# Strassen's method for a second matrix product, with weight blocks fetched again in every batch

## The chip, the cores and the metric

The kernel runs on one core of one Trainium2 chip. The metric is the device time of one execution in microseconds. Three timed executions of the kernel before took 501.92, 504.31 and 504.30 us: the median is 504.3 us.

## The reference

Eight batches of 576 tokens go through block-wise attention (eight heads of 64, blocks of 64 tokens) and then through a gated MLP. The MLP is what the change touches:

```python
h = x @ w_in                       # 576x512 @ 512x1024, then Gelu
u, v = h[..., :512], h[..., 512:]
v_n = (v - mu) / np.sqrt(var + 1e-06) * g_ln
v_s = np.einsum('ts,bsd->btd', w_sg, v_n) + b_sg[None, :, None]
out = x + (u * v_s) @ w_out
```

Inputs and outputs are float32.

## The kernel before

Every float32 operand of a large matmul is held as a high and a low part, and a product is three matmuls (low by high, high by low, high by high). `split` (line 378) makes the parts: a cast on ScalarE, then a subtraction on VectorE or GpSimd. The weights come as 64-bit words and are decoded at the start (`pair_begin`, `pair_end`, lines 443 to 472, for `w_in`; `o_w`, line 511, for `w_out`).

A batch has four stages on TensorE. **v** (`v_unit`, line 817): four units of 128 tokens, 12 matmuls of 512 columns each, and in even batches a fifth unit for the first 64 tokens of two batches together (`xodd`). Then Gelu, a normalization whose reciprocal root GpSimd computes (tile `sm`), and a split into `v` high and low. **u** (`u_unit`, line 856): four units, each 128 of the 512 output rows, 24 matmuls of 288 columns, then one Gelu on ScalarE straight out of PSUM. **s** (`s_unit`, line 883): the token mix with `w_sg`, 28 matmuls a unit, then VectorE multiplies by u and `g_split` makes the parts. **o** (`o_unit`, line 930, for batches 0 and 1; `o_fast`, line 981, for batches 2 to 7).

`o_fast` is Strassen's method in Winograd's form: the 512x512 by 512x576 product is cut into 2x2 blocks, and seven block products stand in place of eight. Its products (`product`, line 947) use 12 matmuls of 288 columns each. They go, in the order 1, 5, 2, 6, 3, 7, 4, through three PSUM tiles; products 6, 7 and 4 add to what product 1 left in tile `a`, and product 3 to what product 5 left in `b`, so each waits until VectorE has read the tile. Three products (3, 6, 7) take sums of weight blocks as the stationary operand, held in two tiles `wx`; a fourth sum replaces block (1,0) of the weights in place. `w_sums` (line 539) makes them once, beside batch 2's u units: sums on GpSimd, splits on ScalarE and VectorE. The moving operand's sums (`ts`) are made by `g_split` and `late_split`.

Attention runs in between on the same engines: scores (`att_scores`, line 648), transposition (`att_transpose`, line 718: VectorE's block transposition, copies on ScalarE and VectorE into `ptT`) and output (`att_out`, line 745), whose result `keep` (line 788) writes as `xf` (whole), `xh` and `xl` (parts). A tile is 128 tokens; nine tiles are two batches. `SLOTS` (line 64) says behind which unit of a batch a tile's step stands in the program, for odd (1) and even (0) batches: "S" scores, "T" transposition, "O" output. `xh`, `xl` of a batch share two buffers with `gh`, `gl` of the same batch (tags `big_0`, `big_1`).

The order on each engine isn't the order of the program. A planner (`Plan`, line 172) records every operation with a cost (`price`, line 131), gets a due time for each by going back from the matmuls (`due`), simulates the engines three times (`run`), and emits the operations in the order of their simulated starts. All are emitted from one line, so the profile gives line 232 for all; groups are told apart by the tiles' names. In a name `pm<-wsg,v` the left is what is written and the right what is read.

`START` (line 45) is the order of steps for loading and decoding weights and for batches 0 and 1; "D11" and "D14" in it are dummy matmuls (`keep_clock`, line 1051), each of which shows as two records `pm<-ident`. `ON_POOL` (line 70) names steps that run on GpSimd in place of VectorE. `REST_V` and `REST_U` (line 82) choose for each piece of `w_in` where its low part is made: "p" on TensorE, "v" VectorE, "g" GpSimd.

Of the kernel before, what the change touches and what calls it, by code (L numbers as in the profile page):

```python
# [20 lines left out]
PSUM = bass.MemoryType.PSUM  # L21

B, H, S, D = 8, 8, 576, 64
P = 128
# [21 lines left out]
A1 L2 L0 A0 B0 B1 L1 S0 T0 A2 A4 W0 A3 D11 W1 L3 S1 W2 S2 S3 w0 w1 W3 T1 O0 w2 O1 T2 w3 D14 T3 S4 M0 O2 v00 X0 O3 G0  # L46
T4 v01 A8 B8 O4 x0 X1 v02 x1 X2 v03 U1 X3 v04 U0 x2 g0 P5 x3 g2 g3 g4 F0 u02 g1 F1 u03 T5 s00 T6 P7 s01 Q5 s02 T7 T8
s03 Q7 v10 v11 Y0 v12 v13 Y2 Y1 u10 Y3 u11 Y4 s10 Y5 s11 Y6 u13 Y7 u12 A10 B10 s12 P9 A12 s13 T9 T10 o02 P11 A14 o01
o03 o00 Q9 B12 T11 o10 T12 o11 B14 S13 A15 o12 T13 Q11 o13
"""  # L50

SUMS = {5: 0, 6: 1, 7: 2, 8: 3}
# [21 lines left out]
FAST = 2  # L74

# [6 lines left out]
REST_V, REST_U = "pppp", "gggg"  # L82
ENGINES = ("tensor", "vector", "scalar", "gpsimd", "sync")
AHEAD = 96
# [8 lines left out]
def cells(a):  # L93

    width = mybir.dt.size(a.dtype)
# [23 lines left out]
class Op:  # L119
    def __init__(self, engine, method, args, kwargs):  # L120
# [7 lines left out]
        self.locks = False  # L128
        self.cost, self.lag = self.price()

    def price(self):
# [3 lines left out]
        if self.engine == "tensor":  # L135
            x = self.ins[-1]
            n = self.outs[0].free_size()
            if x.dtype == F32R:
                return (5.9 if n < 400 else 4.6) + 0.447 * n, 160
            if x.dtype == BF16:  # L140
                return 4.6 + 0.42 * n, 160
            if self.ins[0].ap[0][1] == D:
                return 40, 160
            return (118 if self.method == "transpose" else 1.83 * n + 10), 160
        if self.engine == "sync":
            return (420 if self.ins[0].ap[-1][1] >= P else 620), 2500 + self.ins[0].size() / 100
        wide = [a for a in self.ins if a.free_size() > 1]
        copies = self.method in ("tensor_copy", "tensor_scalar") and n > 1
        if self.engine == "gpsimd":
            self.locks = self.method == "tensor_tensor" and n > 8  # L150
        if self.engine == "vector":
            if self.method == "memset":
                return 600, 80
            self.locks = not psum and (len(wide) > 1 or copies)
# [4 lines left out]
        return (850 if "pow" in str(self.kwargs.get("op")) else 200 + 1.8 * n), 42  # L159
# [10 lines left out]
class Plan:  # L170

    def __init__(self, nc):
        self.nc, self.ops, self.touched = nc, [], {}
        self.tag_of, self.room, self.order = {}, {}, {}
        for e in ENGINES:
            setattr(self, e, Recorder(self, e))
# [13 lines left out]
    def add(self, op):  # L190
        k = len(self.ops)
        self.ops.append(op)
        seen = [(a, True) for a in op.outs] + [(a, False) for a in op.ins]
# [40 lines left out]
    def due(self, users, after, at):  # L234
# [16 lines left out]
        return late  # L251

    def run(self, users, after, at):
# [17 lines left out]
        def begin(k):  # L271
# [4 lines left out]
            for name in op.tiles:  # L276
# [3 lines left out]
                rank = 0 if name == heads[key][0] else 1  # L280
# [4 lines left out]
            if op.engine == "sync":  # L285
                t = max(t, lanes[0])
            if op.locks:
# [5 lines left out]
        for _ in range(len(ops)):  # L293
            best = None
            for e in ENGINES:
                if e == "tensor":
                    while pe < len(tensor) and start[tensor[pe]] is not None:
                        pe += 1
                    ks = [k for k in tensor[pe : pe + AHEAD] if start[k] is None]
# [33 lines left out]
            if op.locks:  # L333
                held[e] = [t, t + cost + op.lag]
# [29 lines left out]
def block_attention_gated_mlp(ctx: ExitStack, tc: tile.TileContext, qkv, w_in, w_out, w_sg, g_ln, b_sg, out):  # L364
# [11 lines left out]
    ps_m = pool("ps_m", 4, space=PSUM)  # L376

# [150 lines left out]
    def w_whole(blk):  # L528

        r = tmp.tile([P, S], F32, name="r", tag="tmp")[:, : 4 * P]  # L530
        hi, lo = (a[:, blk].rearrange("p k e -> p (k e)").bitcast(F32) for a in (wout_h, wout_l))
        nc.gpsimd.tensor_tensor(r, hi, lo, op=ALU.add)
        return r

    def w_split(place, src):
        hi, lo = (a.rearrange("p k e -> p (k e)") for a in place)
        split(hi, lo, src, nc.scalar, nc.vector)

    def w_sums(step):
        nonlocal wx  # L540
        if step == 0:
            wx = [
                blocks_of(const.tile([P, 3 * 4 * P], F32R, name=f"wx_{i}", tag=f"wx_{i}"), 3) for i in range(2)
            ]
            sums["11"], sums["21"] = w_whole(W_BLOCK[0, 0]), w_whole(W_BLOCK[1, 0])
            s3 = tmp.tile([P, S], F32, name="r", tag="tmp")[:, : 4 * P]
            nc.gpsimd.tensor_tensor(s3, sums["11"], sums["21"], op=ALU.subtract)
            w_split([a[:, 1] for a in wx], s3)
        elif step == 1:
            r = w_whole(W_BLOCK[1, 1])  # L550
            nc.gpsimd.tensor_tensor(sums["21"], sums["21"], r, op=ALU.add)
            nc.gpsimd.tensor_tensor(sums["11"], sums["21"], sums["11"], op=ALU.subtract)
            w_split([a[:, 0] for a in wx], sums["11"])
        elif step == 2:
            r = w_whole(W_BLOCK[0, 1])
            nc.gpsimd.tensor_tensor(r, r, sums["11"], op=ALU.subtract)
            w_split([a[:, 2] for a in wx], r)
        else:
            w_split([a[:, W_BLOCK[1, 0]] for a in (wout_h, wout_l)], sums["21"])
# [35 lines left out]
    wout_h = wout_l = wsg_h = wsg_l = wx = None  # L595
# [52 lines left out]
    def att_scores(*tiles):  # L648
# [29 lines left out]
        for i, t in enumerate(tiles):  # L678
            eng = nc.gpsimd if t > last[1] else nc.vector
# [107 lines left out]

    def keep(b, off, n, src, tiles=0, on_pool=False):
        if b not in xf:
            xf[b] = xp.tile([P, HP, S], F32, name="xf")  # L790
            xh[b] = xp.tile([P, HP, S], F32R, name="xh", tag=f"big_{b % 2}")
            xl[b] = xp.tile([P, HP, S], F32R, name="xl", tag=f"big_{b % 2}")
        dst = [a[b][:, :, off : off + n] for a in (xh, xl, xf)]
# [13 lines left out]
        if off == 0:  # L807
            if b % 2 == 0:
# [314 lines left out]
```

## Time and profile before

| what | value |
|---|---|
| median of three timed executions | 504.3 us |
| profiled execution, its own time | 504.54 us |
| its span, first to last instruction | 502.7 us |
| mean granted TensorE clock | 0.995 |
| ScalarE busy | 288.5 us |
| GpSimd busy | 107.1 us |
| moved by DMA | 46.58 MB, mean 93 GB/s |

In the profile, PE is TensorE's matmuls, PEld its weight loads, DVE VectorE, ACT ScalarE, POOL GpSimd and SP the engine that issues DMAs (SPq its queue). A group's row gives shapes (partitions x elements), a count, the busy time of the group, the mean duration in ns, and the idle time just before with what ended it. A row of the timeline gives start and duration in us. A row of a stretch gives its length, busy time and instructions of each engine, the granted clock, the share of DMA and GB/s.

### The profile page before, as it was taken

What the parts mean: (1) busy time and instruction counts of PE and PEld (TensorE: products, weight loads), DVE (VectorE), ACT (ScalarE), POOL (GpSimd) and SP (SyncE); (2) the same over time, 40 slices, a digit from 0 to 9 for tenths busy, and PEclk for the clock granted to TensorE, in tenths of its full rate; (3) what the DMA queues carried; (4) which work ended last, traced back from release to release, by engine and by line L of the source; (5) the groups of instructions that cost most, each with busy time, mean ns of one, the idle gap of its engine ahead of it and who ended that gap; (6) DMA issues with size and microseconds to landing.
All of it is one profiled execution on the core that took longest, in us unless ns stands there. A gap on an engine that the chain in (4) does not pass through costs nothing.

```text
span 502.7 us, 12445 instructions
## 1 busy us (share of the span) xinstructions
PE 487.9 (97%) x5198; PEld 451.6 (90%) x5198; DVE 383.6 (76%) x696; ACT 288.5 (57%) x493; POOL 107.1 (21%) x110
## 2 busy tenths in 40 slices
PE   6899899999999999999999999999999999999996
PEld 5577799899998899988999899988999899998996
DVE  6979889895996886889657796889658786676056
ACT  4988498734464887447731688348742688313120
POOL 0234405375710311013000131013100131002000
PEclk9999899999999999999999999999999999999999
DMA  8974012221436431325111423425121510020002
GB/s 335 358 204 145 0 43 70 61 84 43 169 112 170 140 90 58 108 72 150 38 50 51 150 42 97 116 73 150 24 63 42 157 23 22 2 72 24 1 1 94
DMA packets 52683, 46.58 MB, mean 93 GB/s; under 512 B 35218, under 2 KB 45458, under 8 KB 52628
## 3 DMA queue, kind: packets, MB, share of 16 engines
q1 hardware_dynamic: 52628, 45.80, 30.0%
q8 instruction: 41, 0.67, 0.6%
q14 instruction: 14, 0.11, 0.1%
HBM read 36.34 MB, written 9.44 MB: 91 GB/s over the span
## 4 chain that ended last, share of the span: by engine, by line
PE 66%; DVE 16%; ACT 9%; DMA 4%; issue 3%; POOL 1%; SPq 0%; DVEq 0%; POOLq 0%; ACTq 0%
PE pm L232 66%; DMA qk<-qkv 2%; DVE nmax L232 2%; ACT L232 2%; DVE u L232 2%; DVE wsg L232 1%; DVE sm L232 1%; ACT pt L232 1%; DMA wout<-w_in 1%; DVE v L232 1%; DVE xl L232 1%; ACT ptT L232 1%; DVE gl L232 1%; DVE hs L232 1%; DVE wout L232 1%
## 5 line engine op out<-in xcount | busy, mean ns | idle before, releaser
L232 PE MATMUL pm<-wsg,v 128*128 128x288 f32 x768 | 108.2, 296 | 0.2 <-DVE v L232 0.2
L232 PEld LDWEIGHTS pm<-wsg,v 128*128 128x128 f32 x768 | 103.9, 189 | 0.8 <-DVE v L232 0.4
L232 POOL TENSOR_TENSOR sm<-sm,neg_half 128x1 f32<-128x1 f32 x36 | 33.9, 942 | 166.0 <-DVE sm L232 164.8
L232 ACT COPY ptT<-blocks 32x256 f32<-32x256 f32 (+1 forms) x93 | 44.4, 477 | 25.9 <-DVE blocks L232 23.9
L232 PE MATMUL pm<-xh,win_l 128*128 128x288 f32 x256 | 56.2, 301 | 1.9 <-ACT u L232 1.9
L232 POOL TENSOR_TENSOR pt<-pt,nmax 128x512 f32<-128x512 f32 x27 | 30.7, 1149 | 119.1 <-DVE nmax L232 116.3
L232 PE MATMUL pm<-xl,win_h 128*128 128x288 f32 x256 | 55.7, 299 | 0.0
L232 PE MATMUL pm<-xh,win_h 128*128 128x288 f32 x256 | 55.5, 299 | 0.0
L232 PE MATMUL pm<-gh,wout 128*128 128x288 f32 x272 | 53.1, 296 | 0.0
L232 PE MATMUL pm<-win_h,xl 128*128 128x512 f32 x128 | 51.6, 403 | 0.8 <-ACT hs L232 0.8
L232 PE MATMUL pm<-win_h,xh 128*128 128x512 f32 x128 | 50.7, 396 | 0.0
L232 PE MATMUL pm<-win_l,xh 128*128 128x512 f32 x128 | 50.7, 396 | 0.0
L232 ACT CAST gh<-u 128x576 fp32r<-128x576 f32 x32 | 21.6, 674 | 50.2 <-DVE u L232 50.1
L232 ACT ACT_TABLE_LOAD x32 | 41.1, 1283 | 10.3 <-DVE pt L232 7.7
L232 PEld LDWEIGHTS pm<-xh,win_l 128*128 128x128 f32 x256 | 41.9, 191 | 3.5 <-ACT u L232 2.3
L232 DVE TENSOR_TENSOR u<-pm,u 128x576 f32<-128x576 f32 x32 | 24.1, 753 | 26.4 <-PE pm L232 26.3
L232 PEld LDWEIGHTS pm<-gh,wout 128*128 128x128 f32 x272 | 42.4, 188 | 0.3
L232 PEld LDWEIGHTS pm<-xl,win_h 128*128 128x128 f32 x256 | 41.7, 191 | 0.0
L232 PEld LDWEIGHTS pm<-xh,win_h 128*128 128x128 f32 x256 | 41.7, 191 | 0.0
L232 PE MATMUL pm<-gl,wout 128*128 128x288 f32 x136 | 35.2, 297 | 0.1
L232 ACT ACTIVATE v<-hs,sm 128x512 fp32r<-128x512 f32 x32 | 23.0, 723 | 20.1 <-POOL sm L232 15.8
L232 ACT ACTIVATE hs<-pm 128x512 f32<-128x512 f32 x36 | 21.4, 598 | 22.6 <-PE pm L232 21.7
(130 smaller groups left out, 965.2 us busy)
## 6 DMA issues: line engine op xcount, KB each, us to landing
qk<-qkv SPq DMA_DIRECT2D x31, 512.0 KB, 4.5
out_dram<-ot SPq DMA_DIRECT2D x31, 288.0 KB, 2.4
av<-qkv SPq DMA_DIRECT2D x116, 64.0 KB, 3.2
wsg<-w_in SPq DMA_DIRECT2D x4, 512.0 KB, 9.5
wout<-w_in SPq DMA_DIRECT2D x4, 512.0 KB, 5.3
st<-w_out SPq DMA_DIRECT2D x8, 256.0 KB, 3.1
qkv_w<-qkv SPq DMA_DIRECT2D x2, 768.0 KB, 8.6
stage<-w_sg SPq DMA_DIRECT2D x5, 288.0 KB, 4.0
```

What stands on the lines that cost most here:

```text
L232: getattr(getattr(self.nc, op.engine), op.method)(*op.args, **op.kwargs)
```

## The change

u's product of batches 2 to 7 is made like o's: `u_fast` replaces the four u units by seven products through three PSUM tiles. x's quarters need sums (`x_sums`, after v units 1, 2 and 3), which lie in buffers of the next batch (tag `big_{(b + 1) % 2}`); so the attention results of the next batch come later, by a new `SLOTS`, and the first 64 tokens of an odd batch are first kept in `xodd` alone (`from_aside` copies them over).

The sums of `w_in`'s blocks are made once ("V0" to "V3" in `START`), those of `w_out`'s beside batch 2's s units in place of its u units. There is one pair of `wx` tiles for both. So both sets are stored to DRAM when they are made (from SP's queue), and from batch 3 on each batch fetches u's set during v and o's set at the start of s (from GpSimd's queue). `START` has another order and no dummies ("D0" issues none); `ON_POOL`, `REST_V`, `REST_U`, `ACT_SOFTMAX` move small steps between engines; the planner gets other costs, limits and some earlier due times.

```diff
-A1 L2 L0 A0 B0 B1 L1 S0 T0 A2 A4 W0 A3 D11 W1 L3 S1 W2 S2 S3 w0 w1 W3 T1 O0 w2 O1 T2 w3 D14 T3 S4 M0 O2 v00 X0 O3 G0
+A1 L2 L0 A0 B0 B1 L1 S0 T0 A2 A4 W0 A3 D0 L3 S1 W1 W2 S2 S3 w0 w1 W3 T1 O0 w2 O1 T2 T3 w3 S4 M0 O2 D0 v00 X0 O3 G0 T4
...
-SUMS = {5: 0, 6: 1, 7: 2, 8: 3}
+SUMS = {9: 0, 10: 1, 11: 2, 12: 3}
+X_SUMS = {1: 0, 2: 1, 3: 2}
...
-SLOTS = {
-    1: "0:O01 0:S23 4:T2 5:T3 6:O23 6:S4 8:T4",
-    0: "0:O4 0:S56 3:T5 4:T6 5:O56 5:S78 7:T7 8:T8 9:O78 9:S9A 14:T9 15:TA",
-}
-ON_POOL = ("Y", "Z", "l0", "l2", "l3", "n2",)
-ACT_SOFTMAX = (0, 2, 4)
+SLOTS = {1: "3:T0 6:S23 6:T1 9:O01 10:T2 12:T3 12:S4 13:O23 14:T4", 0: "0:O4 1:S56 5:T5 7:T6 9:S78 9:O56 11:T7 12:T8 14:O78 14:S9A"}
+ON_POOL = ("Y", "a", "c", "l0", "l3", "l4", "n2",)
+ACT_SOFTMAX = (2, 4,)
...
-REST_V, REST_U = "pppp", "gggg"
+REST_V, REST_U = "vppp", "pgvv"
-AHEAD = 96
+EARLY = {'P11': 2, 'x3': 12, 'Y4': 2, 'Y0': 8, 'O4': -4, 'L3': 3, 'v01': 12, 'v04': -4, 'X3': 1, 'O3': -4}
+AHEAD = 10000
+HORIZON = 25000
...
+            split_to(block(1, 0), sums["21"])
+            kept[kind] = [spare.tile([P, 3 * 4 * P], F32R, name=f"kept_{kind}_{i}") for i in range(2)]
+            for a, c in zip(kept[kind], wx[kind]):
+                nc.sync.dma_start(out=a.bitcast(F32), in_=c.rearrange("p n k e -> p (n k e)").bitcast(F32))
...
+    def w_extras(kind):
+        wx[kind] = extras()
+        for a, c in zip(kept[kind], wx[kind]):
+            nc.gpsimd.dma_start(out=c.rearrange("p n k e -> p (n k e)"), in_=a)
...
+    def x_sums(b, n):
+        def quarter(i, j):
+            return xf[b][:, 2 * i : 2 * i + 2, j * HS : (j + 1) * HS]
+        if not n:
+            tx[b] = [
+                xp.tile([P, 4, 2, HS], F32R, name=f"tx_{i}", tag=f"big_{(b + 1) % 2}") for i in range(2)
+            ]
+        eng = pick("t")
+        new = lambda: tmp.tile([P, 2, HS], F32, name="xs", tag="tmp")
+        put = lambda k, t: split(tx[b][0][:, k], tx[b][1][:, k], t, nc.scalar, nc.vector)
+        if n == 0:
+            t = new()
+            eng.tensor_tensor(t, quarter(0, 1), quarter(0, 0), op=ALU.subtract)
+            put(3, t)
+            eng.tensor_tensor(t, quarter(1, 1), t, op=ALU.subtract)
+            put(0, t)
+            sums["x"] = t
...
+    def u_fast(b, step):
...
+        def done(pm, i, j):
+            nc.vector.tensor_tensor(part(i, j), pm[:, :, :HS], part(i, j), op=ALU.add)
+            nc.scalar.activation(part(i, j), part(i, j), AF.Gelu_apprx_tanh, scale=-1.0)
+        if step == 0:
+            u2[0] = mp.tile([P, KT, S], F32, name="u2", tag="u2")
+            o["a"] = new()
+            product("u", b, 1, o["a"], True)
+            nc.scalar.copy(part(0, 0), o["a"][:, :, :HS])
+            o["b"] = new()
+            product("u", b, 5, o["b"], True)
+            nc.scalar.copy(part(1, 1), o["b"][:, :, :HS])
+        elif step == 1:
+            c = new()
+            product("u", b, 2, c, True)
+            done(c, 0, 0)
+            product("u", b, 6, o["a"], False)
+            nc.scalar.copy(part(0, 1), o["a"][:, :, :HS])
+        elif step == 2:
+            product("u", b, 3, o["b"], False)
+            done(o["b"], 0, 1)
+            product("u", b, 7, o["a"], False)
+            done(o["a"], 1, 1)
+        else:
+            product("u", b, 4, o["a"], False)
+            nc.scalar.activation(part(1, 0), o["a"][:, :, :HS], AF.Gelu_apprx_tanh, scale=-1.0)
...
-        units += [(u_unit, i) for i in range(4)]
+        units += [(u_fast if b >= U_FAST else u_unit, i) for i in range(4)]
...
+            if b > FAST and i == 1:
+                w_extras("u")
+            if b > FAST and i == nv + 4:
+                w_extras("o")
...
+            if b >= U_FAST and i in X_SUMS:
+                sooner(x_sums, b, X_SUMS[i])
```

The other two steps of `x_sums` have one difference and one split each.

More of the change, by code (lines that the diff above doesn't have):

```diff
@@ L153, in price @@
                 return 600, 80
-            self.locks = not psum and (len(wide) > 1 or copies)
+            self.locks = self.waits = not psum and (len(wide) > 1 or copies)
             one = len(self.ins) == 1 and not psum and self.method in ("tensor_copy", "tensor_scalar")
@@ L250, in due @@
                 late[k] = min(late[k], late[s] - ops[s].cost - lag)
-        return late
+        return [t - op.early for t, op in zip(late, ops)]
     def run(self, users, after, at):
@@ L298, in run @@
                         pe += 1
-                    ks = [k for k in tensor[pe : pe + AHEAD] if start[k] is None]
+                    ks, span = [], 0.0
+                    for k in tensor[pe : pe + 150]:
+                        if start[k] is None:
+                            ks.append(k)
+                            span += ops[k].cost
+                            if span > AHEAD:
+                                break
                 else:
@@ L526, in block_attention_gated_mlp, with blocks_h_l @@
     sums = {}
[L528 to L540, printed above, removed]
-        if step == 0:
[L542 to L548, printed above, removed]
+    def blocks_h_l(kind):
+        if kind == "o":
+            return lambda i, j: [a[:, W_BLOCK[i, j]] for a in (wout_h, wout_l)]
+        return lambda i, j: [a[:, 2 * j : 2 * j + 2, 2 * i * P : 2 * (i + 1) * P] for a in (win_h, win_l)]
@@ new lines, in extras, with w_sums, new, whole @@
+    def extras():
+        return [blocks_of(const.tile([P, 3 * 4 * P], F32R, name=f"wx_{i}", tag=f"wx_{i}"), 3) for i in range(2)]
+    def w_sums(kind, step):
+        block = blocks_h_l(kind)
+        def new():
+            return tmp.tile([P, S], F32, name="r", tag="tmp")[:, : 4 * P].rearrange("p (k e) -> p k e", k=2)
+        def whole(i, j):
+            r = new()
+            hi, lo = (a.bitcast(F32) for a in block(i, j))
+            pick("c").tensor_tensor(r, hi, lo, op=ALU.add)
+            return r
+        def split_to(place, src):
+            split(place[0], place[1], src, nc.scalar, nc.vector)
+        if step == 0:
+            wx[kind] = extras()
+            sums["11"], sums["21"] = whole(0, 0), whole(1, 0)
+            s3 = new()
+            pick("c").tensor_tensor(s3, sums["11"], sums["21"], op=ALU.subtract)
+            split_to([a[:, 1] for a in wx[kind]], s3)
@@ L549, in w_sums @@
         elif step == 1:
[L550 to L553, printed above, removed]
+            r = whole(1, 1)
+            pick("c").tensor_tensor(sums["21"], sums["21"], r, op=ALU.add)
+            pick("c").tensor_tensor(sums["11"], sums["21"], sums["11"], op=ALU.subtract)
+            split_to([a[:, 0] for a in wx[kind]], sums["11"])
@@ L806, in keep, with from_aside @@
             nc.scalar.copy(dst[2], src)
-        if off == 0:
-            if b % 2 == 0:
-                xodd[0] = [xp.tile([P, HP, 2 * ODD], F32R, name=f"xodd_{i}", bufs=1) for i in range(2)]
-            c = slice(b % 2 * ODD, (b % 2 + 1) * ODD)
-            for dst, src in zip(xodd[0], (xh[b], xl[b])):
-                nc.scalar.copy(dst[:, :, c], src[:, :, 0:ODD].bitcast(F32))
+        if off == 0 and not aside:
+            for a, src in zip(odd_columns(b), (xh[b], xl[b])):
+                nc.scalar.copy(a, src[:, :, 0:ODD].bitcast(F32))
+    def from_aside(b):
+        for a, c in zip(x_parts(b), [x[:, :, ODD:] for x in xodd[0]]):
+            nc.scalar.copy(a[:, :, 0:ODD], c.bitcast(F32))
+    tx = {}
+    def x_sums(b, n):
[15 more added lines that the diff above has]
+            sums["x"] = t
+        elif n == 1:
+            t = new()
+            eng.tensor_tensor(t, quarter(1, 1), quarter(0, 1), op=ALU.subtract)
+            put(1, t)
+        else:
+            t = sums["x"]
+            eng.tensor_tensor(t, quarter(1, 0), t, op=ALU.subtract)
+            put(2, t)
     vh, vl, vs = {}, {}, {}
@@ L1062, in block_attention_gated_mlp, with sooner @@
     for step in START.split():
+        nc.early = 1000 * EARLY.get(step, 0)
         steps[step[0]](int(step[1:]))
+    kinds = {att_scores: "S*", scores: "S*", att_transpose: "T*", outputs: "O*", x_sums: "X*", w_sums: "W*"}
+    def sooner(f, *args):
+        nc.early = 1000 * EARLY.get(kinds[f], 0)
+        f(*args)
+        nc.early = 0
+    nc.early = 0
     for b in range(2, B):
-        units = [(v_unit, m) for m in range(4 if b % 2 else 5)]
-        units += [(u_unit, i) for i in range(4)]
+        nv = 4 if b % 2 else 5
+        units = [(v_unit, m) for m in range(nv)]
+        units += [(u_fast if b >= U_FAST else u_unit, i) for i in range(4)]
         units += [(s_unit, i) for i in range(4)] + [(o_fast, i) for i in range(3)]
```

115 lines of the change are left out of this document (75 added, 40 removed).

## The prediction

> **What bounds the kernel now.** I read the page's engine lines first, then the busy time by batch, then TensorE's instructions in order of time.
>
> ```profile
> span 502.7 us, 12445 instructions
> PE 487.9 (97%) x5198; PEld 451.6 (90%) x5198; DVE 383.6 (76%) x696; ACT 288.5 (57%) x493; POOL 107.1 (21%) x110
> PEclk9999899999999999999999999999999999999999
> ```
>
> TensorE is busy for 97% of the span and VectorE for 76%. A mean says little here, so I asked for the stretches; the columns are PE, PEld, DVE, ACT, POOL busy, granted clock, DMA share, GB/s.
>
> ```profile
> 0.00:31.20 31.20, 24.23 (x342) 18.25 (x342) 25.72 (x57) 21.61 (x64) 3.43 (x8) 1.00 0.91 316
> 31.20:63.80 32.60, 29.82 (x257) 23.67 (x253) 27.91 (x50) 23.58 (x55) 15.18 (x12) 0.95 0.35 100
> 63.80:130.00 66.20, 66.04 (x673) 62.57 (x673) 55.55 (x105) 42.08 (x74) 31.12 (x35) 1.00 0.24 73
> 130.00:160.20 30.20, 30.20 (x418) 29.27 (x417) 26.41 (x45) 16.05 (x28) 8.52 (x7) 1.00 0.43 135
> 160.20:220.40 60.20, 59.34 (x695) 54.81 (x694) 47.89 (x86) 39.05 (x57) 10.14 (x11) 1.00 0.34 97
> 274.50:334.60 60.10, 59.95 (x707) 55.94 (x706) 47.91 (x86) 36.19 (x54) 10.41 (x11) 1.00 0.34 96
> 334.60:388.60 54.00, 54.00 (x565) 51.35 (x565) 40.06 (x73) 31.92 (x47) 7.83 (x8) 1.00 0.26 72
> 447.00:498.80 51.80, 51.80 (x354) 49.40 (x352) 26.75 (x45) 12.11 (x19) 3.76 (x4) 1.00 0.09 30
> ```
>
> The first two rows are the start, the next two batches 0 and 1; then come batch 2, batch 4 (even, five v units), batch 5 (odd, four) and batch 7. From 63.8 us on TensorE has no idle time to speak of: 59.95 of 60.10 us, 54.00 of 54.00. Removing matmuls there shortens the run, as long as nothing else becomes late. VectorE is next: 47.91 of 60.10 in an even batch, 40.06 of 54.00 in an odd one. My baseline is the profiled execution, 504.54 us (span 502.7 and 1.8 around it); the median of the three timed runs, 504.3, is 0.2 below.
>
> **What is removed.** A u unit is 24 matmuls of 288 columns.
>
> ```profile
> 182.22 0.54 PE L232 MATMUL pm<-xh,win_l 128*128 128x288 f32 x2
> ...
> 191.93 3.35 PE L232 MATMUL pm<-wsg,v 128*128 128x288 f32 x24
> 446.97 0.40 PE L232 MATMUL pm<-win_h,xl 128*128 128x512 f32 x1
> 449.77 1.75 PE L232 MATMUL pm<-ts,wout 128*128 128x288 f32 x12
> 451.36 0.40 PE L232 MATMUL pm<-win_h,xl 128*128 128x512 f32 x1
> ```
>
> Between the first two rows stand three u units, nothing else: 72 matmuls in 191.93 - 182.22 = 9.71 us, 0.135 us each. (A row's own duration overlaps the next matmul; only starts can be subtracted.) The other rows give 449.77 - 446.97 = 2.80 us for a v unit and 451.36 - 449.77 = 1.59 us for one Strassen product of 12 matmuls. Four u units are 96 matmuls; seven products of 12 are 84. So 12 go in each of six batches, 72 in all: again **9.71 us** off TensorE, all on the path.
>
> **What each batch gains on the other engines.** These rows have the same shapes as the added work.
>
> ```profile
> L232 DVE TENSOR_TENSOR u<-u 128x576 f32<-128x576 f32 x18 | 13.6, 754 | 0.2
> L232 DVE TENSOR_TENSOR ts<-u,ts 128x576 fp32r<-128x576 f32 x18 | 13.5, 753 | 0.2
> L232 DVE TENSOR_TENSOR u<-pm,u 128x576 f32<-128x576 f32 x32 | 24.1, 753 | 26.4 <-PE pm L232 26.3
> L232 ACT CAST ts<-u 128x576 fp32r<-128x576 f32 x18 | 11.6, 674 | 23.3 <-DVE u L232 23.3
> L232 ACT ACTIVATE u<-pm 128x576 f32<-128x576 f32 x32 | 20.5, 647 | 10.0 <-PE pm L232 9.7
> ```
>
> VectorE: four differences of x's quarters, four subtractions for their low parts, three additions in u's end: 11 x 0.753 = 8.3 us. ScalarE: four casts of 0.674 and three copies out of PSUM at about 0.647: 4.6 us; the four Gelus stay. In an even batch ScalarE then has 40.8 of about 58.5 us, which TensorE hides. VectorE is the question. Batches 4 and 5 together: 47.91 + 40.06 + 16.6 = 104.5 us of work in 60.1 + 54.0 - 3.2 = 110.9 us, that is 94%. The even one alone has 56.2 in 58.5, but the softmax of the next pair's first tiles is due only in the odd batch's transposes, so some work can slip over. Can VectorE run so densely without holding TensorE up?
>
> ```profile
> 280.50:291.90 11.40, 11.40 (x57) 9.18 (x50) 10.39 (x22) 9.06 (x14) 4.44 (x5) 1.00 0.49 142
> 281.90:298.30 16.40, 16.40 (x204) 14.21 (x203) 15.58 (x33) 13.69 (x21) 5.81 (x6) 1.00 0.32 89
> 324.20:334.60 10.40, 10.25 (x75) 9.70 (x74) 10.10 (x19) 2.64 (x5) 1.56 (x2) 1.00 0.09 30
> ```
>
> It ran at 91%, 95% and 97% here. The last is the o stage, whose seven products pass through the same three PSUM tiles as the new u stage, each waiting for the read of the one before; TensorE lost 0.15 us in it. That is my low end: five loaded batches (2 to 6) x 0.15 = 0.8 us; batch 7 has room. High end: at 91%, 104.5 / 0.91 = 114.8, which is 3.9 us over for a pair, 9.8 us for the five. I take **3.0 us**, nearer the o stage since its products are built the same way. A gain below nothing is excluded: nothing here gets lighter.
>
> x's sums use the buffers where the next batch's attention results went, so those move to the s and o stages (the new SLOTS). They are the same instructions on the same queues, and where VectorE lags the price is already in the 9.8. Their new wait, x's sums needing the whole batch's tokens, ends behind v's second unit, with at least two v units and one product, 2 x 2.80 + 1.59 = 7.2 us, still ahead of the first use.
>
> **Weight blocks.** The sums for u come early, in the stretch of batches 0 and 1, and o's sums move from u's units of batch 2 to its s units.
>
> ```profile
> L232 POOL TENSOR_TENSOR r<-r 128x512 f32<-128x512 f32 x4 | 6.0, 1512 | 0.3
> L232 DVE TENSOR_TENSOR wx<-r,wx 128x512 fp32r<-128x512 f32 x3 | 3.9, 1303 | 0.0
> L232 DVE TENSOR_TENSOR u<-u 128x288 f32<-128x288 f32 x12 | 5.5, 457 | 0.3
> qk<-qkv SPq DMA_DIRECT2D x31, 512.0 KB, 4.5
> qkv_w<-qkv SPq DMA_DIRECT2D x2, 768.0 KB, 8.6
> ```
>
> Eight GpSimd sums at most 1.512 us each (12.1 us) fit the idle GpSimd. Four VectorE subtractions are at most 1.303 us, 5.2 us; in the old run such sums were done before 160 us, so u's take their place there and o's come on top in batch 2: 47.89 + 8.3 + 5.2 = 61.4 us against 60.2 - 1.6 = 58.6, 2.8 us over. Part slips into batch 3: I take **1.0**, bounds 0 and 2.8. Four stores of 768 KB go on SP's queue, ahead of qk and v loads; each holds the transfer engines for up to 8.6 us, but the loads are issued two tiles ahead. I take 0; without that cover one qk load would be late by up to 8.6.
>
> From batch 3 on, GpSimd's queue issues two 768 KB loads for u, later two for o. They wait for the last product that reads the old blocks; behind them wait v's reciprocal roots, and behind those ScalarE's v, due only in the s stage. For u they must land before product 6: four v units (11.2), the last o product and three u products (4 x 1.59 = 6.4) make 17.6 us, 20.4 in an even batch. No GpSimd load is in this trace. By the SP rows the pair takes 9 us (as two qk loads, quicker for being smaller) to 17.2 us (two of 768 KB one after the other, in the crowded start). I take 12, hidden: 0.
>
> **Start and batches 0 and 1.** "Z" moves 16 sums of 256 columns from GpSimd to VectorE, at most 0.457 us each, 7.3 us: 62.9 of 66.2 us in that stretch. Hidden, 0; at 91% density it would cost 2.9. The start has this wait:
>
> ```profile
> L232 PE MATMUL pm<-ident 128*128 128x128 f32 x50 | 9.1, 335 | 2.4 <-ACT ident L232 2.4
> 31.25 0.50 PE L232 MATMUL pm<-win_h,xl 128*128 128x512 f32 x1
> 52.81 2.33 POOL L232 TENSOR_TENSOR sm<-sm,neg_half 128x1 f32<-128x1 f32 x1 [2.16 <-DVE sm L232]
> 55.17 0.72 ACT L232 ACTIVATE v<-hs,sm 128x512 fp32r<-128x512 f32 x1 [3.72 <-POOL sm L232]
> 56.48 0.54 PE L232 MATMUL pm<-xh,win_l 128*128 128x288 f32 x2 [1.91 <-ACT u L232]
> 54.50:61.40 6.90, 4.99 (x26) 4.85 (x26) 5.42 (x14) 3.56 (x6) 2.17 (x3) 0.75 0.00 0
> ```
>
> The first v unit begins at 31.25. Later a slow root on GpSimd delays ScalarE, which delays TensorE by 1.91 us, and then the granted clock is 0.75 over 6.90 us: 1.7 us more. The new order, with less of the weights' low parts on GpSimd (REST_U), may remove these 3.6 us. Against it: the 25 dummies (50 records) kept the clock up in the first 31 us. They fill waits, so taking them out gains nothing; without them the first v unit may run at half clock, 2.80 us more, and three or four more VectorE operations there at about 0.75 cost up to 3.0. I take **-1.0**, bounds -3.6 and +5.8.
>
> [...]
>
> **Sum:** 504.54 - 9.71 + 3.0 + 1.0 - 1.0 = **497.8 us**, own range 493.5 to 501.5.
>
> **Rivals.** *VectorE becomes the bound* (91% reached, not 95): 504.54 - 9.71 + 9.8 + 1.0 - 1.0 = 504.6, no change. For: it must stay as dense over whole batches as it was over 16 us. Against: TensorE's end of each stage leaves slack, and 97% was seen. Worse density (88%) gives 104.5 / 0.88 - 110.9 = 7.9 per pair, 19.7 in all, 514.
>
> [...]
>
> *All is hidden and the start's wait goes*: 504.54 - 9.71 + 0.8 - 3.6 = 492.0. *The start loses what the batches gain* (+5.8 and 2.9 there): 497.8 + 6.8 + 2.9 = 507.5, or about half of it, 502.7: no change.
>
> **How the numbers follow.** A difference under 0.5% (2.5 us) can't be told from none. Chances: forecast 0.52, all hidden 0.14, VectorE bound 0.18 (0.12 of it no change, 0.06 slower), blocks late 0.10 (slower), start 0.06 (no change). Faster 0.66, same 0.18, slower 0.16. The range 491.5 to 506 leaves out the late blocks, the dense tail and a little below.
>
> **What would show it.** Right: TensorE at 12 fewer matmuls per batch, an even batch near 58.5 to 59.5 us and an odd one near 52.5 to 53.5, VectorE at 92 to 96% of them, product 6 of u waiting for no DMA. Wrong: TensorE idle before u products with a release by VectorE or ScalarE (density), by DMA on wx (late blocks), or a first v unit much after 31 us (start).

## The result and the profile after

The changed kernel takes 508.34 us (median of 20 executions, 504.24 to 515.6); the kernel before, 503.93 us in 20 executions beside it (501.92 to 505.48). The ratio is 1.0083 with the interval 1.0063 to 1.0103: 0.8% slower; it leaves out the two slowest executions of the changed kernel (512.42 and 515.6), which lie over 1.5% above its quickest. The forecast was 497.8 us, 10.5 us too low; the range ended at 506.

The profiled execution of the changed kernel is the quickest of the 20, 504.24 us. Its page first; the last two rows are DMA issues (KB each, median us from issue to landing).

```profile
span 502.3 us, 12336 instructions
PE 478.3 (95%) x5069; PEld 436.9 (87%) x5076; DVE 434.2 (86%) x785; ACT 308.5 (61%) x520; POOL 109.4 (22%) x120
PE 41%; DVE 38%; ACT 8%; DMA 8%; issue 3%; POOL 1%; SPq 0%; DVEq 0%; ACTq 0%; POOLq 0%
out_dram<-ot SPq DMA_DIRECT2D x31, 288.0 KB, 2.5
wx<-kept_u POOLq DMA_DIRECT2D x10, 768.0 KB, 7.1
```

The matmuls went: 5069 in place of 5198, which is 72 of u, 50 records of the dummies and a few records that are missing. But TensorE now idles more, VectorE rose from 76% to 86%, and 8% of the chain that ended last is DMA. Next the stretches that answer to those of the prediction: the start, batch 2, batch 4, batch 5, batch 7.

```profile
0.00:27.60 27.60, 15.49 (x246) 10.36 (x250) 21.39 (x45) 14.96 (x41) 3.01 (x8) 1.00 0.73 267
155.80:218.90 63.10, 60.38 (x684) 54.05 (x681) 56.22 (x98) 43.45 (x68) 21.88 (x18) 1.00 0.41 133
272.90:332.70 59.80, 58.77 (x694) 54.26 (x693) 53.74 (x96) 39.93 (x63) 11.19 (x13) 1.00 0.43 131
332.70:387.60 54.90, 53.64 (x554) 50.10 (x553) 47.91 (x86) 34.22 (x51) 10.80 (x13) 1.00 0.46 146
446.10:498.60 52.50, 50.88 (x342) 47.98 (x340) 35.21 (x60) 17.65 (x28) 5.68 (x8) 1.00 0.29 95
```

The start won 3.65 us here (first v unit at 27.60, before at 31.25). Batch 2 lost 2.9. Batches 3 to 7 should each have shrunk by 1.62 us (12 matmuls of 0.135) and didn't: batch 4 went from 60.1 to 59.8, batch 5 from 54.0 to 54.9, batch 7 from 51.8 to 52.5. TensorE lacks about 1.3 us in batch 5 and 1.6 in batch 7, where it lacked nothing before. From the first v unit of batch 3 to the end of batch 7 it is 279.6 us, before 278.4.

In batch 7 the trail can be followed. It begins with a wait that is on no list of suspects in the prediction: VectorE waits for an output store. First the stores (SP's queue) of this stretch in the changed kernel, in the view of one tile.

```profile
L242 SPq DMA_DIRECT2D out_dram<-ot x4: 372/386/401, 445.4 to 457.3; - x4
  DVE ot L242: 3.0, 1
DMA to landing us min/median/max: 2.2/2.4/8.4
```

The same view of the kernel before:

```profile
L232 SPq DMA_DIRECT2D out_dram<-ot x3: 372/373/401, 446.4 to 452.3; - x3
DMA to landing us min/median/max: 2.2/2.2/2.3
```

And the changed kernel in order of time (start, us, engine, instruction, idle before it and what ended it), GpSimd, VectorE and TensorE:

```profile
446.32 1.12 POOL L242 DMA_DIRECT2D wx<-kept_u  x2 [11.91 <-PE pm L242]
452.75 0.75 DVE L242 TENSOR_TENSOR tx<-xs,tx 128x576 fp32r<-128x576 f32 x1
456.49 0.76 DVE L242 TENSOR_TENSOR ot<-pm,xf 128x576 f32<-128x576 f32 x1 [2.99 <-DMA out_dram<-ot]
464.15 1.87 PE L242 MATMUL pm<-tx,wx 128*128 128x288 f32 x12 [0.27 <-ACT u L242]
468.90 1.87 PE L242 MATMUL pm<-tx,wx 128*128 128x288 f32 x12 [1.29 <-ACT u L242]
```

At 446.32 GpSimd issues the two fetches. A store of batch 6's output goes out on SP's queue just behind them and lands after 8.4 us in place of 2.2. Its source is one of four `tmp` buffers, which x's sums, v's Gelu output, the attention's blocks and the o stage's results share. So VectorE, which needs a buffer for `ot` at 453.5, stands for 2.99 us. VectorE's later operations are late too, ScalarE's behind them, and seven and twelve microseconds on, products 6 and 7 of u wait for ScalarE's copy out of their PSUM tile, 1.56 us together. (Over the whole run VectorE waits for such stores twice, 4.6 us, and ScalarE twice, 3.3 us; in the run without a fetch, below, neither does.) The fetched blocks themselves were there in time:

```profile
L242 POOL DMA_DIRECT2D wx<-kept_u x2: 535/563/591, 446.3 to 446.9; - x2
DMA to landing us min/median/max: 5.9/7.4/8.9
```

The second landed 8.9 us after 446.9, at 455.8; product 6 began at 464.15.

### The profile page after: what moved, and what is told of

Read it like the earlier page. It is cut to its first block, busy times and chain, and to the rows that moved or that the text cites. A ratio compares the mean times of both kernels' runs of the same rounds, so it can differ in the third digit from the quotient of the medians.

```text
span 502.3 us, 12336 instructions
## 1 busy us (share of the span) xinstructions
PE 478.3 (95%) x5069; PEld 436.9 (87%) x5076; DVE 434.2 (86%) x785; ACT 308.5 (61%) x520; POOL 109.4 (22%) x120
## 4 chain that ended last, share of the span: by engine, by line
PE 41%; DVE 38%; ACT 8%; DMA 8%; issue 3%; POOL 1%; SPq 0%; DVEq 0%; ACTq 0%; POOLq 0%
PE pm L242 39%; DMA out_dram<-ot 6%; DVE u L242 5%; DVE nmax L242 4%; DVE sm L242 4%; DVE ot L242 3%; DVE hs L242 3%; DVE v L242 3%; DVE tx L242 3%; DVE xs L242 2%; DVE pt L242 2%; PE banks L242 2%; DVE blocks L242 2%; DVE ptT L242 2%; DMA av<-qkv 1%
## 5 line engine op out<-in xcount | busy, mean ns | idle before, releaser
L242 POOL TENSOR_TENSOR sm<-sm,neg_half 128x1 f32<-128x1 f32 x36 | 30.9, 858 | 133.8 <-DVE sm L242 124.7
L242 ACT COPY ptT<-blocks 32x256 f32<-32x256 f32 (+1 forms) x93 | 44.2, 475 | 23.4 <-DVE blocks L242 21.6
L242 PE MATMUL pm<-win_h,xl 128*128 128x512 f32 x128 | 51.8, 405 | 0.0
L242 DVE TENSOR_TENSOR u<-pm,u 128x576 f32<-128x576 f32 x50 | 36.8, 747 | 13.0 <-PE pm L242 12.5
L242 DVE TENSOR_TENSOR ot<-pm,xf 128x576 f32<-128x576 f32 x32 | 23.9, 748 | 9.9 <-DMA out_dram<-ot 3.0
L242 DVE BATCH_NORM_STATS2 sm<-hs 128x6 f32<-128x512 f32 x36 | 24.7, 686 | 6.4 <-ACT hs L242 6.4
L242 PEld LDWEIGHTS pm<-win_h,xh 128*128 128x128 f32 x128 | 24.0, 188 | 5.9
L242 PEld LDWEIGHTS pm<-win_h,xl 128*128 128x128 f32 x128 | 24.0, 188 | 5.4
L242 PEld LDWEIGHTS pm<-win_l,xh 128*128 128x128 f32 x128 | 24.1, 188 | 4.9
L242 PE MATMUL pm<-xh,win_l 128*128 128x288 f32 x112 | 27.9, 296 | 0.0
L242 PE MATMUL pm<-xl,win_h 128*128 128x288 f32 x112 | 27.9, 296 | 0.0
```

The source lines that it names most:

```text
L242: getattr(getattr(self.nc, op.engine), op.method)(*op.args, **op.kwargs)
```

## The experiments

**What the fetch costs.** Theory: the fetches hold up the stores behind them, the stores hold buffers. Rivals: VectorE's density; late blocks. The first run emits no fetch and lets products 3, 6 and 7 of batches 3 to 7 read the blocks that batch 2 left, so u's weight sums are replaced by w_out's; the order of all else is kept. The second issues u's fetches behind the batch's first reciprocal root on GpSimd's queue.

```diff
 no_fetch, in Plan.emit:
+    if op.method == "dma_start" and op.engine == "gpsimd":
+        continue
+    if op.resident is not None:            # matmuls of products 3, 6, 7
+        op.args = (op.args[0], op.resident, *op.args[2:])
...
 late_fetch, in Plan.emit:
+    if op.method == "dma_start" and op.engine == "gpsimd" and "kept_u" in op.kwargs["in_"].tensor.name:
+        held.append(op)
+        continue
...
+    if op.engine == "gpsimd" and op.kwargs.get("op") == ALU.pow:
+        for x in held:
+            self.nc.gpsimd.dma_start(**x.kwargs)
```

> Left out: the fetch of the weight blocks in batches 3 to 7; products 3, 6 and 7 there read the blocks of w_out made in batch 2, for u as well, so the sums are of other data. The order of all other instructions is the changed kernel's. Stores theory: stores go back to 2.3 us, VectorE no longer waits for a store, 496 to 501 us, and the spread of the runs falls from 6 us to about 2. Density theory (VectorE at 92 to 95% is too dense, the fetch is hidden): 505 to 509, spread unchanged.

> u's two fetches are issued behind the reciprocal root of the batch's first v unit, some 6 us later, in place of ahead of it; all else in the same order. Stores theory: the batch's last stores are out before the fetch, 498 to 503 us. Density theory: no change, 505 to 509. Late-block theory (the fetch itself is awaited): slower, 510 to 515, since it lands later.

Without the fetch: 500.84 us, ratio 0.9931 (0.9912 to 0.995). Batches 3 to 7 last 53.23, 59.29, 53.22, 57.40 and 50.32 us, 273.5 together, 6.1 less than in the changed kernel. Counted from the start of each of TensorE's matmuls to the next one's start, most of this lies in the u stages: 56.7 us for the five, 62.1 in the changed kernel. The result is in the range of the stores theory, and the executions lie within 1.5 us of each other. Issued later: 503.35 us, 0.9979 (0.9958 to 1.0), 0.35 us above that theory's range. Batches 3 to 6 are then as without a fetch, but batch 7 is 52.72: there the last store still comes behind the fetch, lands after 6.8 us, and u's products wait 1.88 us.

Is it the buffers, or the traffic? A fifth `tmp` buffer decides it, with the fetch left where it was and the order planned for four.

```diff
...
-    tmp = pool("tmp", 4)
+    tmp = nc.pool(ctx.enter_context(tc.tile_pool(name="tmp", bufs=5)), 4)
...
-    low = [const.tile([P, P], BF16, name=f"low_{i}") for i in range(2)]
+    low = 2 * [const.tile([P, P], BF16, name="low")]
...
-    g_bc = const.tile([P, DH], F32, name="g_bc")
+    g_bc = win_h[:, 0, DH:].bitcast(F32)
...
```

> The changed kernel with five buffers for the shared temporary tiles in place of four, the order of instructions as planned for four; the room comes from leaving out the normalisation's gain (a row of w_in's weights stands in for it) and one of the two scaled unit matrices, so the values are wrong. Stores theory (the fetch hurts because the stores behind it hold buffers that VectorE and ScalarE need): batches 3 to 7 within 0.4 of those without a fetch (53.2, 59.3, 53.2, 57.4, 50.3), median 500 to 502 with the late rise of the clock. Rival (the fetch hurts through the memory's traffic, or through late blocks): as in the changed kernel, 54.0, 59.8, 54.9, 58.5, 52.4, median 507 to 509.

Measured 502.06 us, 0.9958 (0.9933 to 0.9983). Its stores between 443 and 460 us:

```profile
DMA to landing us min/median/max: 2.3/3.3/8.4
```

VectorE's instruction that had waited 2.99 us, now without a wait:

```profile
451.50 0.75 DVE L244 TENSOR_TENSOR ot<-pm,xf 128x576 f32<-128x576 f32 x1
```

And batches 3, 5 and 7:

```profile
222.20:275.40 53.20, 53.20 (x554) 50.03 (x553) 49.10 (x88) 32.89 (x51) 10.99 (x13) 1.00 0.46 144
334.70:387.90 53.20, 53.20 (x554) 50.08 (x553) 48.05 (x86) 32.91 (x50) 10.80 (x13) 1.00 0.48 151
445.50:495.90 50.40, 50.36 (x342) 47.92 (x340) 35.29 (x60) 17.88 (x28) 5.68 (x8) 1.00 0.30 99
```

A store still takes 8.4 us, but VectorE no longer waits 2.99 us for it. Its first addition in u's end, at 464.08, begins 18.6 us after the batch's first v unit; in the changed kernel, at 467.74, 21.6 us. TensorE is full, and batches 3 to 7 last 273.7 us, within 0.2 of the run without a fetch. The fetch's transfers cost nothing; the buffers held by the delayed stores cost all of its 6 us. This is shown. Why a store is slow behind a fetch is not: no run here separates the ways in which two queues could share the transfers. In the five profiles of the changed kernel each output store that was issued within 1.1 us behind the second fetch, and whose landing is on record, landed 0.2 to 0.8 us behind that fetch. In the first of them there are three, issued at 274.63, 334.40 and 447.96 us: they took 7.1, 8.5 and 8.4 us and landed 0.6, 0.2 and 0.6 us behind it.

**Does the same fetch hurt without the new u stage?** The new start and planner with the old u units were run alone, and then with w_out's blocks stored and fetched again in batches 3 to 7.

```diff
 start_alone, against the changed kernel:
-U_FAST = 2
+U_FAST = 8
 (old SLOTS, old SUMS, no V steps, no w_extras)
 fetch_alone, against start_alone:
+            if b > FAST and i == 1:
+                w_extras("o")
```

> The new start, planner and small moves alone: u of batches 2 to 7 by the old units, the old places of attention and of w_out's sums, no fetch and no stores of blocks. If the 4.4 us that the first profile shows gained before batch 2 are the start's own: 499 to 501 us. If they are only borrowed (work pushed into later batches): 503 to 505.

> u by its old units; the new start, prices and planner as in the run with the start alone, plus w_out's sums stored once and fetched again (two of 768 KB, GpSimd's queue) once in each of batches 3 to 7, at the place of u's fetch. Stores theory: the output store issued behind the fetch lands after 5 us or more in place of 2.3, VectorE or ScalarE waits for its buffer; how much reaches TensorE is open, since plain u units take no tmp buffers: 0.2 to 1.2 us a batch, median 505 to 510. Rival (the fetch costs only because u's products wait on the copies that the buffers hold up): 503.5 to 505.

The start alone: 504.15 us, 0.9994 (0.9975 to 1.0014), as expected of a gain that is only borrowed: in its profile batch 2 begins 1.1 us earlier than before and lasts 1.6 us longer. With the fetch: 503.28 us, 0.9996 (0.9974 to 1.0018), though a store lands after 7.2 us there too.

```profile
L245 SPq DMA_DIRECT2D out_dram<-ot x4: 372/386/401, 271.6 to 280.4; - x4
DMA to landing us min/median/max: 2.2/3.7/7.2
```

No engine is listed as waiting for it; here are no x sums that want a buffer, and no products of u that hang on VectorE. The stores theory expected 505 to 510 here and missed; the rival had it. So the cost needs both parts of the change, the fetch and the new u stage.

**Has VectorE any reserve?** In the run without a fetch, the four subtractions for x's low parts were emitted twice in batches 3 to 7 (3.0 us each), and the four for w_out's sums twice in batch 2.

```diff
+                for _ in range(op.times):   # 2 for these subtractions
                     getattr(getattr(self.nc, op.engine), op.method)(*op.args, **op.kwargs)
```

> The kernel without a fetch (products 3, 6 and 7 of u read w_out's sums in batches 3 to 7, which leaves u's values wrong), with the four VectorE subtractions for the low parts of x's sums done twice in batches 3 to 7 (3.0 us more VectorE work in each), and the four for w_out's sums done twice in batch 2 (about 5 us more). Density theory: VectorE binds the steady batches, so each grows by 1.5 to 3 us and the median is 508 to 516. Slack theory: VectorE's density costs nothing there, each grows by under 0.4, 500.8 to 502.8 if batch 2 is unchanged too. For batch 2: if its extra 2.7 us come from VectorE's sums, it grows from 62.8 by 2 us or more; if from the order of other work, by under 0.7.

519.23 us, 1.0316 (1.0284 to 1.0347): slower than even the density theory expected. From the list of TensorE's waits (us in total, times, longest; the same row of the changed kernel has 3.8 us, and the run without a fetch, on which this one builds, has no such row):

```profile
PE pm L248 <- ACT u L248: 12.0, 6, 2.8
```

Batches 3 and 5 of the same run:

```profile
224.60:280.60 56.00, 53.58 (x555) 50.14 (x554) 52.10 (x92) 33.29 (x51) 8.58 (x9) 1.00 0.26 79
343.00:399.40 56.40, 53.82 (x555) 50.15 (x554) 50.89 (x90) 34.03 (x51) 8.58 (x9) 1.00 0.30 87
```

3.0 us more VectorE work made these batches 2.7 to 3.2 us longer, by the same wait that the changed kernel shows, though VectorE is busy for 93% and 90% of them. Nearly all of it lies in the u stage, 11.4 us without the added work and 13.9 and 14.3 with it. Batches 6 and 7 grew by 5.4 and 3.7 us, 6.8 and 3.4 us of them at half clock, though VectorE is busy for only 71% of batch 7. At its present load it costs nothing there (53.20 of 53.20 above), but ahead of u's products it has no reserve: what it loses there, TensorE loses. So a 3 us wait for a buffer could come through.

**How late may the fetch be, and do dummies help the start?** The changed kernel with eleven dummies at TensorE's front, nothing else altered; and the same with u's fetch behind the batch's second root.

```diff
-A1 L2 L0 A0 B0 B1 L1 S0 T0 A2 A4 W0 A3 D0 L3
+A1 L2 L0 A0 B0 B1 L1 S0 T0 A2 A4 W0 A3 D11 L3
```

> The changed kernel with the first eleven dummy matmuls put back at TensorE's front and nothing else altered. Clock theory (without dummies TensorE runs at half clock until about 18.8 us in some executions and 27.5 us in others, worth 3.4 us): the granted clock is full before 10 us, the first v unit begins at 27.0 to 28.0 in every execution, batches 0 to 7 last as in the changed kernel, and the median is 503.5 to 505.5 with a narrow spread. Rival (eleven dummies at the front don't hold the clock over the idle gaps that follow): the median stays at 507 to 508.5 and the spread stays wide.

> The eleven dummies, and u's two fetches issued behind v1's root on GpSimd's queue, so behind the batch's last output store; else the changed kernel. Stores theory with clock theory: no output store waits behind the fetch, batches 3 to 7 last as without a fetch (62.8 for batch 2 stays; 53.2, 59.3, 53.2, 57.4, 50.3 to 50.8), the fetches land before product 6 needs them, the first v unit begins at 27.0 to 28.0: median 497 to 499.5, faster than both kernels. Late-block theory: u's product 6 or 3 waits for a DMA on wx, a microsecond or more in batches 3, 5 and 7. If the dummies do nothing: 500.5 to 501.5.

509.31 us, 1.0117 (1.0082 to 1.0153), and 511.71 us, 1.0161 (1.0136 to 1.0186): the clock theory failed in the first and the stores theory in the second. In the first the clock was full from 6.7 us, but fell to half again from 13.5 to 20.3. In the second run the rival of late blocks came true in batches 3 and 5 (58.4 and 57.6 us). TensorE in batch 3:

```profile
241.45 0.37 PE L247 MATMUL pm<-tx,wx 128*128 128x288 f32 x1 [1.66 <-DMA wx<-kept_u]
243.41 1.98 PE L247 MATMUL pm<-tx,wx 128*128 128x288 f32 x11 [1.58 <-DMA wx<-kept_u]
```

The stretch behind it:

```profile
244.60:248.00 3.40, 3.40 (x16) 3.40 (x15) 0.00 (x0) 1.83 (x3) 0.57 (x1) 0.50 0.00 0
```

3.2 us of waiting, and then 3.4 us at half clock, which cost 1.7 more, as much as the half clock of batch 0 in the prediction; and this with the fetch two roots behind the place where the change issues it. Batch 3 took 58.4 us where it took 53.2 with the fetch behind the first root: between too early for the stores and too late for product 6 lies one root.

Next both groups of dummies, round which the planner moves some steps of the start; and the same with the fetch behind the first root, in batch 7 behind the second.

```diff
-A1 L2 L0 A0 B0 B1 L1 S0 T0 A2 A4 W0 A3 D0 L3 S1 W1 W2 S2 S3 w0 w1 W3 T1 O0 w2 O1 T2 T3 w3 S4 M0 O2 D0 v00 X0 O3 G0 T4
+A1 L2 L0 A0 B0 B1 L1 S0 T0 A2 A4 W0 A3 D11 L3 S1 W1 W2 S2 S3 w0 w1 W3 T1 O0 w2 O1 T2 T3 w3 S4 M0 O2 D14 v00 X0 O3 G0 T4
```

> The changed kernel with both groups of dummies put back in START (eleven at the front, fourteen ahead of the first v unit; the planner moves some steps of the start round the second group). Clock theory: with the second group the granted clock stays full from about 6.5 us on, the first v unit begins at 27.5 to 28.8 us in every execution, and the median is 504 to 506. Rival (the new order of the start leaves gaps that no group of dummies covers): half clock again between 12 and 27 us, median 508 or more.

> Both groups of dummies, and u's two fetches issued behind v0's root in batches 3 to 6 and behind v1's root in batch 7. Stores theory with clock theory: 497.5 to 500, faster than both kernels. If the dummies don't hold the clock: 501.5 to 504. If the fetch is late behind v0's root already: TensorE waits on wx in batch 3 or 5.

511.16 us, 1.015 (1.0119 to 1.0181), and 508.21 us, 1.0086 (1.0058 to 1.0114): the rival again in the first, and above every figure expected in the second. There batches 4 to 6 are as without a fetch (59.3, 53.2, 57.5), but batch 3 is 0.8 us longer (54.1), batch 7 1.1 us (51.4), and batch 2 took 65.9 us in place of 62.8, with 6.8 us at half clock; against the run without a fetch the start and batch 0 lost 2.8 us together. Two stretches of the start in the kernel before, and the longest wait of TensorE in them:

```profile
6.40:13.00 6.60, 5.05 (x108) 3.06 (x108) 5.27 (x12) 3.16 (x18) 0.00 (x0) 1.00 1.02 414
13.00:20.00 7.00, 4.84 (x80) 3.17 (x78) 6.62 (x16) 6.95 (x25) 0.00 (x0) 1.00 1.00 338
9.96 1.13 PE L232 MATMUL pm<-wsg,ident 128*128 128x512 f32 x2 [1.49 <-DVE wsg L232]
```

And in the kernel with both groups:

```profile
5.50:12.40 6.90, 3.28 (x110) 2.85 (x108) 3.91 (x8) 1.03 (x2) 0.00 (x0) 1.00 1.02 415
12.40:26.00 13.60, 9.22 (x100) 5.42 (x89) 11.46 (x22) 8.18 (x27) 0.98 (x1) 0.50 0.53 196
11.31 0.66 PE L242 MATMUL banks<-ident,first_pts 128*128 128x128 f32 x4 [3.62 <-DVE first_pts L242]
16.38 1.01 PE L242 MATMUL pm<-wsg,low 128*128 128x512 bf16 x2 [3.70 <-ACT win_h L242]
```

In the old kernel TensorE is busy for 77% and 69% and the clock stays full; with the dummies in the new order it is busy for 48%, and half clock follows for 13.6 us. The means hide another difference: it stands still for 3.62 us in one piece just ahead of the fall and for 3.70 us soon behind it, where the old kernel never waits longer than 1.49 us. The first v unit then began at 38.3 us; batch 0 is 4.2 us shorter in return. START of the kernel before, dummies and all, did worse under the new planner; the second of these runs has the edit of the last experiment too.

```diff
-START = """ the changed kernel's """
+START = """ that of the kernel before, V0 V1 V2 V3 behind o01 """
```

> The changed kernel with START of the kernel before, dummies and all (u's four weight sums behind step o01). Clock theory (the old order of the steps and its dummies hold the clock; the new order holds it neither with dummies nor without): full clock from about 6.5 us on, the first v unit at 30.5 to 31.5 us, batches 2 to 7 as in the changed kernel, median 506 to 508.5 with a spread under 3 us. Rival (chance alone): half clock again after 12 us in some executions, spread as wide as the changed kernel's.

> Both edits: results stored in place, and START of the kernel before. Both theories: batches 3 to 7 as without a fetch, the start as in the kernel before, 499.5 to 501.5 with a spread under 3 us. If the old start alone loses the clock too: 501 to 505.

518.75 us, 1.0248 (1.0203 to 1.0294), and 509.01 us, 1.0083 (1.0052 to 1.0113), both above every figure expected: half clock for 17.1 us of the start in both, and again at the end of batch 1 (6.8 and 3.4 us). In the first run the wait for `first_pts` is the same 3.62 us, so under the new planner the old START doesn't bring the old order back.

**Why is the median 4 us above the profiled execution?** The changed kernel was timed once more and profiled three more times, unchanged.

> The changed kernel once more, unaltered, for a second profile beside the quickest of its runs. All theories: 504 to 511 us, median about 508. Stores theory: in a slower run the output stores issued just behind the 1.5 MB fetch at a batch's start take longer than the 7 to 8.5 us of the first profile, and TensorE's idle time in u grows with them. Density theory: the stores take the same, and the extra time lies in VectorE's own chain.

> The changed kernel as it is, one profiled execution more. Clock theory: the first v unit begins either at 27.4 to 28.2 us (full clock from about 19 us, 504 to 505.5 in all) or at 30.5 to 31.5 us (full clock from 26 to 28.5 us, 507 to 509.5), and the batches after it last the same within 1 us. Rival (the executions above 507 lose their time in the batches): the first v unit at 27.5 us in all.

> As the look before: one of the two starts, and the time follows it.

> As the two looks before: one of the two starts, and the time follows it.

Timed again: 507.74 us, 1.0072 (1.0043 to 1.0101). The three further profiled executions took 508.73, 506.37 and 507.47 us. The same two matmuls of the start, and then the first v unit, in the second and in the third of them:

```profile
21.31 1.12 PE L242 MATMUL pm<-wsg,ident 128*128 128x512 f32 x2
27.61 0.48 PE L242 MATMUL pm<-win_h,xl 128*128 128x512 f32 x1
```

```profile
22.54 2.07 PE L242 MATMUL pm<-wsg,ident 128*128 128x512 f32 x2
30.50 0.48 PE L242 MATMUL pm<-win_h,xl 128*128 128x512 f32 x1
```

Same instructions, same order, and 1.12 against 2.07 us: by the trace's record of the clock it became full at 18.8 us in the one and at 26.4 in the other (before its first entry the views print 1.00). That is worth 2.9 us. Of thirteen profiled executions with this start and no dummies, four rise at 18.8 to 20.1 us and nine at 26.3 to 28.2. The rest of the spread is batches 3 to 7: 281.5, 282.2 and 280.0 us in the three (279.6 in the first profile), and in two of them batch 3 alone took 56.4 and 56.6. So theory and rival each had a part.

**Batch 2.** The four subtractions for w_out's sums on GpSimd, in the kernel with the fetch behind the first root:

```diff
+                if op.lows:
+                    op.engine = "gpsimd"
```

> The kernel with u's fetch behind v0's root, with the four subtractions for the low parts of w_out's sums on GpSimd in place of VectorE (batch 2), the order as planned. VectorE theory of batch 2: it shrinks from 62.85 to 60 to 61.3 us, the other batches as before, median 501 to 502.3. Rival (the moved attention steps and sums wait on other things): 62.3 or more, or longer if GpSimd's sums now come late, median 503 to 505.

503.14 us, 0.9987 (0.9963 to 1.0011), and batch 2 took 63.6 us, not 62.85: no gain. With VectorE's subtractions doubled it took 65.4 instead of 62.8. It was 61.8 with the start alone, 60.2 before. So 1.6 us came with the new planner's assignment and order, and 1.0 net with u's products there. The stages, counted as above, say where: u takes 11.3 us in place of 13.0, as forecast, but v 15.8 in place of 14.2 and s 16.7 in place of 15.1, s already 16.6 with the start alone. VectorE has a share, but which part of the 2.6 us that these add is its, stays open. In the second run with the old START batch 2 took 59.3 us, and batch 1 74.6 in place of 70.3, 3.4 us of it at half clock: part of the extra can move ahead of batch 2.

**A version that beats both.** If the delayed stores hurt only by the buffers that they hold, the o stage needs none: its results can be added into `xf` in place and stored from there.

```diff
     def o_part(pm, base, ot=None, es=slice(0, 2)):
         if ot is None:
-            ot = tmp.tile([P, 2, HS], F32, name="ot", tag="tmp")
+            ot = base
```

> The changed kernel with the o stage's results added into the batch's own x tile and stored from there, so that no store holds a buffer of the shared temporary tiles; the planner orders the rest anew. Stores theory: stores still land after 5 us or more behind a fetch, VectorE doesn't wait for them, batches 3 to 7 last 53.2, 59.3, 53.2, 57.4 and 50.3 us or less, median 499 to 502 as with a fifth buffer, faster than both kernels. Rival (the fifth buffer helped by more room for the other tiles): batches 3 to 7 stay within 0.3 of 54.0, 59.8, 54.9, 58.5, 52.4, median 506 to 508.

499.49 us (498.51 to 502.49), ratio to the kernel before 0.9917 (0.9891 to 0.9944). Its stores between 442 and 450 us, and then its batches 5 and 7:

```profile
DMA to landing us min/median/max: 2.3/3.6/8.3
```

```profile
332.00:385.20 53.20, 53.20 (x553) 50.04 (x553) 48.67 (x86) 32.98 (x50) 12.04 (x13) 1.00 0.50 153
442.90:493.70 50.80, 50.62 (x342) 47.95 (x340) 35.52 (x60) 18.08 (x28) 5.68 (x8) 1.00 0.30 98
```

The stores are as slow as ever, and the change pays: 0.8% faster than before, with the early fetch and without dummies. Batches 3 to 7 last 274.6 us, 1.1 more than without a fetch; ScalarE now waits for stores of `xf` itself, 3.9 us in two places.

## Why the prediction was wrong

**Removed matmuls, 9.71 us:** right.

**VectorE's density, +3.0:** right in size, by luck. Without the fetch's cost, batches 3 to 7 gained 278.4 - 273.7 = 4.7 of 8.1 us; 3.4 are lost. But VectorE doesn't hold TensorE up there: with the fifth buffer TensorE idles in neither batch 3 nor 5, and batch 7, which has no attention beside it, gained 1.5 of 1.62. Counted by stages, batch 5's u went from 13.0 to 11.4 us, all that was forecast, while the same matmuls of s took 0.2 us more, those of o 0.3 and those of attention 0.3. So the loss lies in the stages into which the attention steps moved. The prediction had put their price into VectorE's. What makes those matmuls longer wasn't tested. The rival of VectorE as the bound was wrong as stated, but near: ahead of u's products there was no reserve.

**Fetched blocks, 0: the step that failed.** The prediction put this term at 0 because the blocks land before product 6 needs them. They did: 9.5 us after the first issue in batch 7, where it had taken 12. It didn't ask what else is in flight beside them, whose source those transfers hold, and who needs it. That cost 6.0 us (279.6 against 273.7), more in the slower profiles. For the four stores of the blocks it had asked which loads they delay; for the fetch it had named only what is queued behind it on GpSimd. The output stores go by SP's queue, and still landed behind it, by 0.2 to 0.8 us.

**Batch 2, +1.0 (0 to 2.8):** mis-sized, and outside its bounds. It should have been 60.2 - 1.6 = 58.6 us without extra work; it was 62.9 with a fifth buffer, 4.3 more. 1.6 of this the start and the planner add alone; the sum had no term for them in batch 2.

**Start, -1.0 (-3.6 to +5.8):** -1.6 in most executions, inside its bounds, and -4.4 in the first profile, past the lower one; the reason was partly foreseen. Without dummies half clock holds until 18.8 to 20.1 us or 26.3 to 28.2; the first v unit comes at 27.5 to 28.2 or 30.5 to 31.2 (before: 31.25), so the start gains 3.1 to 3.8 us or 0.1 to 0.8, and batches 0 and 1 another 0.8. The wait of 1.91 us in batch 0 and the half clock behind it are gone, as hoped, but batch 0 is only 0.3 us shorter in the first profile: work that stood ahead of the first v unit now stands in it. The half clock ended ahead of the first v unit, so the 2.80 us feared for it weren't paid. That the dummies had kept the clock up in the kernel before was an estimate: no run took them out there. In the new order eleven of them gave full clock from 6.7 us on, but half clock from 13.5 to 20.3, and both groups half clock from 12.4 to 26.0.

With the measured sizes: 504.5 - 9.7 + 3.4 + 4.3 + 6.0 - 1.6 (late rise) = 506.9, and 504.1 with the early rise, against 504.24 profiled and 508.34 in the median; the rest of the median fits the fetch's larger cost in the later profiles, 0.4 to 2.6 us more in batches 3 to 7.

## What to carry to other kernels

When a change adds a large transfer, list every small transfer that will be in flight beside it, and for each the buffer that it holds and the engine that wants the buffer next; the large one may be hidden and still stop an engine through a small one, as here VectorE for 2.99 us. A result that can be stored from a tile with a long life should not sit in a shared temporary. An engine at 90%, or even 71%, in the mean can have no reserve in one stage: double one of its operations there and see whether the stage grows by as much.

## What the runs showed of the hardware

A store of 288 KB took 2.2 to 2.3 us in the kernel before (446.4 to 452.3 us), and 7.1 to 8.5 us in the changed kernel's first profile when issued on another queue 0.9 to 1.1 us behind the second of two fetches of 768 KB (6.6 to 9.6 us over all profiles).

The clock's rise in the start differed between executions of the same program by 7.6 us (18.8 and 26.4). The stretches between two changes of the clock are multiples of 3.413 us: 51.20, 3.41 and 440.32 us in the kernel before (15, 1 and 129 times), 484.69 us in the changed kernel's first profile (142 times), and the stretches of half clock named above last 3.4, 6.8, 13.6 and 17.1 us. So one can ask how busy TensorE was in the last 3.41 us before a fall, and in such windows that kept full clock. Two of the kernel before, a kept one and the one ahead of its fall at 57.6 us:

```profile
13.26:16.67 3.41, 2.02 (x67) 1.66 (x65) 3.16 (x8) 3.36 (x12) 0.00 (x0) 1.00 1.06 415
54.22:57.63 3.41, 1.50 (x10) 1.15 (x9) 2.14 (x4) 2.31 (x5) 0.91 (x1) 1.00 0.00 0
```

Behind the window of 59% the clock stayed full, behind the one of 44% it was half for 3.41 us. The fall after the 1.66 and 1.58 us waits followed a window of 46%, the one with both groups of dummies a window of 31%, and one in the run with both groups and the later fetch a window of 69%; with eleven dummies a window of 46% kept full clock. So the share alone didn't decide: falls followed windows of 31, 44, 46 and 69%, and full clock those of 46 and 59%.
